# Three units of the first layer's last two groups by seven half-size products, in an attention and feed-forward kernel

## The chip, the cores and the metric

The kernel runs on one core of a Trainium2 chip. The metric is the device time of one execution in microseconds (us). Before the change four runs gave a median of 373.8 us (373.31 to 373.93). Engines: PE is the tensor engine (PEld its weight loads), DVE the vector engine, ACT the scalar engine, POOL the GpSimd engine, SP the engine that issues most transfers.

## The reference

```python
# q, k, v: (8 batches, 8 heads, 576 rows, 64); bias_table: (32, 8)
scores = 1/8 * q @ k.T + bias_table[bucket(|i - j|)]        # per batch and head
attn   = exp(scores - max) / (sum(exp(scores - max)) + 1e-9)
x      = (attn @ v) laid out as 4608 rows of 512
h      = np.maximum(x @ w_in, 0.0)                          # w_in: 512 x 2048
out    = (h * h) @ w_out                                    # w_out: 2048 x 512, out in float32
```

## The kernel before, in words

**Stages.** Attention runs over 32 pairs of heads (`pair`, four per batch). A pair makes scores on PE into two PSUM sets of two banks each (`sets_ps`, ring `r_set`), ACT takes their exponentials into one of three rooms in SBUF (`pt_sb`, ring `r_pt`), DVE multiplies in the bias bands, PE multiplies by v into the bank `pv_ps` (ring `r_pv`), DVE normalises into `xs`, and SP transposes that by DMA into `xt_sb`. The feed-forward runs over nine groups of 512 rows (`layers(g)`, g = 0 to 8). Layer 1 of a group is 16 blocks of 128 hidden units: four matmuls 512 wide per block (L1094) into one of three PSUM banks (`g_ps`, ring `r_g`), an ACT relu out of PSUM into one of four buffers `rts` (L1115), a DVE square into `gs` (L1125). Layer 2 (`second(g)`) is done by seven products of half-size blocks in place of eight: DVE sums of the squared activations (`sums_of_activations`, L971, in two chunks of four operations), each product as two runs of eight matmuls 256 wide (L1012), and evictions by ACT copies (L1045) or DVE multiply-and-adds (L1039) into `ys`, from where SP writes rows of the output (L1065).

**Order.** A planner (`Plan.schedule`) puts all operations in order before the kernel is emitted. It takes the operation that can start earliest by its own model of times; among those on one engine that can start at the same time the one with the smallest `due` goes first. The order it finds is fixed on every engine. Layer 1 of group g has dues from 60000 + 39000 g in steps of 2000; the products of `second(g - 1)` lie between them; evictions have due 0, squares the group's due less 100000, sums of activations the group's due less 50000.

**The end.** Group 7 needs rows of the last batch, group 8 only such rows. So layer 1 of groups 7 and 8 and layer 2 of groups 7 and 8 come behind the last pair. Before, the order of the seven products in the last group was

```python
P_ORDER = "1 2 6 5 7 3 4"
P_LAST = "1 6 2 5 7 3 4"
```

where products 1 and 2 need only squares, product 6 the second sum (s2, for which the first sum s1 is needed), 5 the first, 7 the third and 3 the fourth. Products 1 and 2 add up in one bank "a".

Of the kernel before, what the change touches and what calls it, by code (L numbers as in the profile page):

```python
# [10 lines left out]
FP32 = mybir.dt.float32  # L11
FP16 = mybir.dt.float16
EXPF = mybir.ActivationFunctionType.Exp
RELUF = mybir.ActivationFunctionType.Relu
COPYF = mybir.ActivationFunctionType.Copy
MULT = mybir.AluOpType.mult

# [18 lines left out]
QUIET, LATER = 5000.0, 9000  # L36
TAB, EV = 2700.0, 1
P_ORDER = "1 2 6 5 7 3 4"
P_LAST = "1 6 2 5 7 3 4"
SIX = 2  # L40
V_EARLY, V_HW = 18900.0, 2
T_POOL, T_DUE = 0, 0
ORDER = "k0 i0 q1 q0 v i1 o0 k1 i2 o1 o2 i3 o3"
HALF = GT // 2
# [135 lines left out]
def mm(n):  # L180
    return n / 2.4 + 2.5
# [6 lines left out]
def dve(n, rate=1.0, fix=160.0):  # L188
    return fix + n / (0.96 * rate)
# [3 lines left out]
def kernel(  # L193
# [415 lines left out]

    xt_ready, x_last = {}, {}  # L610
    x_bufs = {}

    def copy_to(engs_n, out_f, in_f, deps, bufs, due, fp16=True, dve_only=False):

# [13 lines left out]
    def pair(p):  # L628
# [190 lines left out]
        for part, qt0, nq in ((0, 0, 3), (1, 3, 2)):  # L819
            bank = Buf(r_pv)  # L820

            def pv(qt0=qt0, nq=nq, bank=bank):
                ps = pv_ps[bank.slot][:, 0 : nq * 130].rearrange("p (t e d) -> p t e d", t=nq, e=2)
                pt, pm = pts[pb.slot], p4s[pb.slot]
                va, vm = vas[b_v[b].slot], v4s[b_v[b].slot]
                for i in range(nq):
                    c = (qt0 + i) * 128
                    io(
                        nc.tensor.matmul(  # L829
                            ps[:, i, :, :], pm[:, c : c + 128], vm[:, hp, :, 0:65], start=True, stop=False  # L830
                        )
                    )
                    for e in range(2):
                        for jt in range(4):
                            io(
                                nc.tensor.matmul(  # L836
                                    ps[:, i, e, :],
                                    pt[:, (2 * jt + e) * S + c : (2 * jt + e) * S + c + 128],
                                    va[:, jt, 2 * hp + e, 0:65],
                                    start=False,  # L840
                                    stop=(jt == 3 and e == 1),
                                )
                            )

            o = P.add(
                {"PE": nq * 300.0}, pv,
                bands + list(exps.values()) + l_v[b, hp] + first, [bank, pb, b_v[b]], T + 1, after, "f",
            )
            rb = Buf(r_r)

            def recip(nq=nq, bank=bank, rb=rb):
                ps = pv_ps[bank.slot][:, 0 : nq * 130].rearrange("p (t e d) -> p t e d", t=nq, e=2)
                io(nc.vector.reciprocal(out=rs[rb.slot][:, 0:nq], in_=ps[:, :, :, 64:65]))

            def norm(nq=nq, bank=bank, rb=rb, qt0=qt0):
                ps = pv_ps[bank.slot][:, 0 : nq * 130].rearrange("p (t e d) -> p t e d", t=nq, e=2)
                io(
                    nc.vector.tensor_tensor(  # L858
                        out=xs[xb.slot][:, qt0 : qt0 + nq, :].rearrange("p t (e d) -> p t e d", e=2),
                        in0=ps[:, :, :, 0:64],  # L860
                        in1=rs[rb.slot][:, 0:nq].to_broadcast([128, nq, 2, 64]),
                        op=MULT,
                    )
                )

            o = P.add({"DVE": 200.0}, recip, [o], [bank, rb], T - 2000)
            o = P.add({"DVE": dve(nq * 128)}, norm, [o], [bank, rb, xb], T - 2000)
            norms.append(o)
            if b >= DT_X:
                c = (b % XB) * S + 128 * qt0  # L870
                t = P.add(
                    {"SP": 1320.0},
                    lambda qt0=qt0, nq=nq, c=c: io(
                        nc.sync.dma_start_transpose(
                            out=xt_sb[:, hp, c : c + 128 * nq].rearrange("p (t d) -> p t d", d=128), in_=xs[xb.slot][:, qt0 : qt0 + nq, :].rearrange("p t d -> p (t d)")
                        )
                    ),
                    [o, x_last.get((hp, 1 - part))] + xt_free(b * S + 128 * (qt0 + nq)), [xb], T - 2000,
                )
                t = x_last[hp, part] = P.add({"DMA": 232.0 * nq}, None, [t], [xb], -1e9)  # L880
                end = b * S + min(128 * (qt0 + nq), S) - 1
                for g_ in range((b * S + 128 * qt0) // GT, end // GT + 1):
                    xt_ready.setdefault(g_, []).append(t)
# [48 lines left out]
    def sums_of_weights():  # L932
# [21 lines left out]
            done.append(o)  # L954
        return done

    def sums_of_activations(g):

        gb = g_bufs[g]
        sb_ = s_bufs[g] = {i: Buf(r_s[i]) for i in (1, 2, 4)}  # L960
        for c0 in (0, 4):
            o = None
            for to, uses in ((1, [1]), (2, [1, 2]), (4, [2, 4]), (3, [])):

                def add(to=to, c0=c0):
# [5 lines left out]
                    io(nc.vector.tensor_tensor(out=out_, in0=a, in1=b_, op=mybir.AluOpType.subtract))  # L971

                o = P.add(
                    {"DVE": dve(1024, 2.0)}, add, squares[g][2 * c0 : 2 * c0 + 8] + [o],
                    [gb] + [sb_[i] for i in uses], G0 + GP * g - 5e4,
                )
                s_done.setdefault((g, to), []).append(o)
# [1 line left out]
    def second(g):  # L979

        gb, sb_ = g_bufs[g], s_bufs[g]
        bank = {i: Buf(r_g) for i in ("a", "b", "c", "d0")}
        bank["d1"] = Buf(r_g) if g == NG - 1 else bank["d0"]
        y = {i: Buf(r_y) for i in ("u", "v", "11", "12")}
        rows_ = out[ds(g * GT, GT), :].rearrange("(s t p) c -> t p s c", s=2, t=2)
        prod = {
            1: ("a", lambda c, s: fourth(gb, 0, 0, c, 1)[:, 0, s], lambda c: w4[:, c, 0, 0], []),
            2: ("a", lambda c, s: fourth(gb, 1, 0, c, 1)[:, 0, s], lambda c: w4[:, c, 1, 0], []),
            3: ("c", lambda c, s: ss[4][:, c, s], lambda c: w4[:, c, 1, 1], [4]),
            4: ("d", lambda c, s: fourth(gb, 1, 1, c, 1)[:, 0, s], lambda c: wt_sb[:, 2, c], []),  # L990
            5: ("c", lambda c, s: ss[1][:, c, s], lambda c: w4[:, c, 0, 1], [1]),
# [10 lines left out]
        atoms = []  # L1002
        for i in (int(x) for x in (P_LAST if g == NG - 1 else P_ORDER).split()):
            bk, left, right, ns = prod[i]
            apart = bk == "d" and g == NG - 1
            for s_ in range(2):
                bf = bank[f"d{s_}" if bk == "d" else bk]

                def mul(i=i, s_=s_, bf=bf, left=left, right=right, apart=apart):
                    for c in range(8):  # L1010
                        io(
                            nc.tensor.matmul(  # L1012
                                g_ps[bf.slot][:, ts(s_, HALF)], left(c, s_), right(c),
                                start=(c == 0 and (s_ == 0 or apart) and i not in before), stop=(c == 7),
                                skip_group_check=True,
                            )
                        )

                def atom(d, i=i, s_=s_, bf=bf, ns=ns, mul=mul):
                    deps = d + [x for n in ns for x in s_done[g, n]] + squares[g]  # L1020
                    deps += read_of[before[i]] if i in before else []
                    deps += l_wout if i in (1, 2) else t_done
                    return P.add(
                        {"PE": 8 * mm(HALF)}, mul, deps, [bf, gb] + [sb_[n] for n in ns if n != 3], 1e6, 0.0, "f",
                    )
# [2 lines left out]
                if s_ == 0 and not apart:  # L1028
                    continue

                def fin(o, i=i, bf=bf, s0=s_ if apart else 0, n=1 if apart else 2):
                    to, plus, where = reads[i]
                    cs = ds(s0 * HALF, n * HALF)

                    def ev():
                        dst, ps = ys[y[to].slot][:, cs], g_ps[bf.slot][:, cs]
                        if plus is not None:
                            io(
                                nc.vector.scalar_tensor_tensor(  # L1039
# [8 lines left out]

                    deps = [o]
                    if plus == "u":  # L1050
                        deps += read_of[1 if i == 6 else 6]
                    if plus == "v":
                        deps += read_of[5]
                    if i == 4:
# [18 lines left out]
                atoms.append(fin)  # L1073
        return atoms

    def layers(g):

        due = G0 + GP * g
# [2 lines left out]
        if g < NG:  # L1081
            g_bufs[g] = Buf(r_gb)
            gb1 = g_bufs[g]
            squares[g] = []
            for nt in range(16):
                bank = Buf(r_g)

                def f1(nt=nt, bank=bank):
# [10 lines left out]
                            )  # L1099

                atoms1.append((nt, f1, bank))
        i2 = 0
        last = None
        for i in range(16):
            if i < len(atoms1):
                nt, f1, bank = atoms1[i]
                o = P.add(
                    {"PE": 4 * mm(512)}, f1, xt_ready[g] + [l_win[nt // 4]], [bank, gb1], due + i * 2000, 0.0, "f"
                )
# [3 lines left out]
                def relu(o, bank=bank, rb=rb):  # L1113
# [4 lines left out]

                engs = {"ACT": act(512), "DVE": dve(512)} if g < RELU_DVE else {"ACT": act(512)}
                r = one_of(engs, relu, [o], [bank, rb], 0.0)  # L1120
                squares[g].append(
                    P.add(
                        {"DVE": dve(512, 2.0)},
                        lambda rb=rb, nt=nt, gb1=gb1: io(
# [6 lines left out]
                )  # L1131
            if i2 < len(atoms2):
                o = atoms2[i2]([last] if last is not None else [])
                o.due = due + i * 2000 + 1000
                last = o
                i2 += 1
                if i2 < len(atoms2) and atoms2[i2].__name__ == "fin":
                    atoms2[i2](o)
                    i2 += 1
# [49 lines left out]
```

The softmax here doesn't subtract the row's maximum and nothing guards it: scores larger than these inputs give would overflow.

## Time and profile before

| | before |
|---|---|
| median of four runs | 373.8 us |
| profiled execution, time | 374.81 us |
| profiled execution, span from first to last instruction | 373.0 us |
| granted PE clock, mean over the span | 0.995 |
| last run of matmuls of exponentials by v begins | 312.65 us |
| first layer-1 matmul of group 7 begins | 315.35 us |
| 315.35 to 357.00: busy PE, PEld, DVE, ACT | 41.65, 25.10, 24.09, 19.70 us |
| last DVE eviction begins | 369.97 us |

Times below are microseconds from the start of the profiled span. A row of groups gives line, engine, operation, output and input, shapes and count, then busy time, mean ns of one instruction, and the idle time of the engine in front of it with its releaser. A row of the chain of waits gives start, length and what ran. Records of PE overlap: a matmul's record is longer than the step from one to the next, and the steps are read from the chain.

### The profile page before, as it was taken

The page shows a single profiled execution, that of the slowest core. Times are in us where ns is not written, and L with a number is a line of the kernel's source. Part 1 is how long each engine was busy: PE and PEld are TensorE (multiplying, and loading weights), DVE is VectorE, ACT ScalarE, POOL GpSimd, SP SyncE. Part 2 cuts the span into 40 slices and gives each one's busy share as a digit, 9 for nine tenths or more (in the row PEclk, how much of TensorE's full clock was granted, in tenths as well). Part 3 has the DMA queues.
Part 4 walks back from the last instruction along what each step waited for, and adds up shares of the span by engine and source line. Part 5 has one row for each costly group of instructions (what it writes and reads, how often), then busy time and mean ns, then how long its engine had stood idle before and what let it go on. Part 6 is the DMA issues. An engine that isn't in the chain of part 4 may idle for free.

```text
span 373.0 us, 9912 instructions
## 1 busy us (share of the span) xinstructions
PE 356.9 (96%) x3930; PEld 243.1 (65%) x3930; DVE 265.6 (71%) x593; ACT 258.1 (69%) x368; POOL 184.2 (49%) x343
## 2 busy tenths in 40 slices
PE   3988999899999999999999999999999999999996
PEld 2656555656687557877785468745877688456775
DVE  3897799958785598658865697579765985583663
ACT  4988889688585886689766887688659870564330
POOL 7896358495665495666846557758413100000000
PEclk9999999999999999999999999999999999999999
DMA  9999999795998989998999899999975122100103
GB/s 171 145 133 160 171 187 105 100 111 78 190 139 108 161 133 143 138 151 155 127 138 136 112 162 128 141 176 154 88 118 129 47 55 66 56 2 28 58 28 114
DMA packets 162292, 44.25 MB, mean 119 GB/s; under 512 B 145734, under 2 KB 162246, under 8 KB 162246
## 3 DMA queue, kind: packets, MB, share of 16 engines
q0 software_dynamic: 74208, 14.53, 49.9%
q1 hardware_dynamic: 87696, 28.80, 41.1%
q8 instruction: 31, 0.51, 0.6%
q10 hardware_dynamic: 342, 0.30, 0.3%
q14 instruction: 15, 0.12, 0.1%
HBM read 36.88 MB, written 9.44 MB: 124 GB/s over the span
## 4 chain that ended last, share of the span: by engine, by line
PE 84%; DVE 6%; ACT 4%; DMA 3%; issue 1%; POOL 0%; SPq 0%; ACTq 0%
PE f L1094 33%; PE f L1012 28%; PE pv L836 8%; PE st L701 8%; PE pv L829 2%; DMA kt<-ks 2%; PE st L750 2%; DVE pt L793 2%; PE st L725 1%; DMA g<-in_q_dram 1%; ACT pt L712 1%; DVE x L858 1%; PE f L656 1%; DVE s L971 1%; ACT pm L760 1%
## 5 line engine op out<-in xcount | busy, mean ns | idle before, releaser
L712 ACT ACTIVATE pt<-st 128x1024 f16<-128x1024 f32 x128 | 127.3, 1023 | 31.5 <-PE st L701 31.5
L1094 PE MATMUL f<-xt,w_in_sb 128*128 128x512 f16 (+4 forms) x704 | 138.6, 341 | 0.2 <-ACT xt L618 0.2
L1115 ACT ACTIVATE rt<-f 128x512 f16<-128x512 f32 x144 | 85.2, 601 | 49.2 <-PE f L1094 45.2
L1094 PEld LDWEIGHTS <-w_in_sb 128*128 128x128 f16 x704 | 62.6, 98 | 57.3 <-issue 12.2
L1125 DVE TENSOR_TENSOR g<-rt 128x512 f16<-128x512 f16 x144 | 63.7, 446 | 36.1 <-ACT rt L1115 35.1
L793 DVE TENSOR_TENSOR pt<-pt,tb_sb 128x1536 f16<-128x1536 f16 (+2 forms) x96 | 60.7, 642 | 15.1 <-ACT pt L712 14.5
L1012 PEld LDWEIGHTS <-g 128*128 128x128 f16 x576 | 54.6, 98 | 14.4 <-issue 4.7
L275 POOL DMA_DIRECT2D qs<-in_q_dram x79 | 55.3, 714 | 5.1 <-DMA w_out_sb<-in_moe_w_out_dram 2.6
L275 POOL DMA_DIRECT2D ks<-in_k_dram x79 | 55.2, 702 | 1.1 <-issue 1.0
L836 PE MATMUL pv<-va,pt 128*128 128x65 f16 x1280 | 55.3, 194 | 0.0
L836 PEld LDWEIGHTS <-pt 128*128 128x128 f16 x1280 | 50.7, 98 | 3.1 <-issue 1.3
L1039 DVE SCALAR_TENSOR_TENSOR y<-f,y 128x512 f32<-128x512 f32 (+1 forms) x47 | 31.4, 667 | 24.1 <-PE f L1012 22.4
L1012 PEld LDWEIGHTS <-s 128*128 128x128 f16 x432 | 41.1, 98 | 10.5 <-issue 2.7
L701 PE MATMUL st<-qt,kt 64*128 64x512 f16 x256 | 40.9, 391 | 0.9 <-ACT pt L735 0.4
L683 POOL COPY qz<-kt 64x64 f16<-64x64 f16 x58 | 19.8, 342 | 39.8 <-DMA kt<-ks 30.2
L1012 PE MATMUL f<-w_out_sb,g 128*128 128x256 f16 x288 | 36.2, 273 | 0.7 <-ACT y L1045 0.7
L683 POOL COPY qz<-qt 64x64 f16<-64x64 f16 x61 | 16.9, 277 | 39.9 <-DMA qt<-qs 26.4
L829 PE MATMUL pv<-vm,pm 128*128 128x130 f16 x160 | 35.5, 222 | 1.0 <-DVE x L858 1.0
L1012 PE MATMUL f<-wt,g 128*128 128x256 f16 x288 | 36.2, 273 | 0.0
L1012 PE MATMUL f<-w_out_sb,s 128*128 128x256 f16 x288 | 36.1, 273 | 0.0
L858 DVE TENSOR_TENSOR x<-pv,r 128x384 f16<-128x384 f32 x64 | 31.4, 490 | 2.0
L971 DVE TENSOR_TENSOR s<-g,s 128x1024 f16<-128x1024 f16 x36 | 26.1, 724 | 0.4
(64 smaller groups left out, 283.5 us busy)
## 6 DMA issues: line engine op xcount, KB each, us to landing
out_dram<-y SPq DMA_DIRECT2D x34, 256.0 KB, 2.3
f<-in_v_dram SPq DMA_DIRECT2D x24, 256.0 KB, 4.2
qs<-in_q_dram POOLq DMA_DIRECT2D x48, 64.0 KB, 4.0
ks<-in_k_dram POOLq DMA_DIRECT2D x48, 64.0 KB, 3.5
w_in_sb<-in_moe_w_in_dram POOLq DMA_DIRECT2D x4, 512.0 KB, 7.3
w_out_sb<-in_moe_w_out_dram POOLq DMA_DIRECT2D x4, 512.0 KB, 10.4
qs<-in_q_dram POOLq DMA_DIRECT2D x7, 144.0 KB, 4.5
ks<-in_k_dram POOLq DMA_DIRECT2D x7, 144.0 KB, 6.0
```

Source lines behind the costliest of these rows:

```text
L275: lambda: io(eng.dma_start(out=out_(), in_=in_())),
L683: io(eng.tensor_copy(out=dst[qb.slot][rw, rw], in_=src[qb.slot][rw, 512:576]))
L701: nc.tensor.matmul(sets_ps[st.slot][:, e, :], kt[rw, ts(jt, 128)], qt[rw, 0:512], start=True, stop=True,)
L712: nc.scalar.activation(out=p5(pts[pb.slot])[:, jt, :, 0:512], in_=sets_ps[st.slot], func=EXPF, scale=SCALE)
L793: io(nc.vector.tensor_tensor(out=a, in0=a, in1=t, op=MULT))
L829: nc.tensor.matmul(ps[:, i, :, :], pm[:, c : c + 128], vm[:, hp, :, 0:65], start=True, stop=False)
L836: nc.tensor.matmul(ps[:, i, e, :], pt[:, (2 * jt + e) * S + c : (2 * jt + e) * S + c + 128], va[:, jt, 2 * hp + e, 0:65], start=False, sto ...
L858: nc.vector.tensor_tensor(out=xs[xb.slot][:, qt0 : qt0 + nq, :].rearrange("p t (e d) -> p t e d", e=2), in0=ps[:, :, :, 0:64], in1=rs[rb.s ...
L1012: nc.tensor.matmul(g_ps[bf.slot][:, ts(s_, HALF)], left(c, s_), right(c), start=(c == 0 and (s_ == 0 or apart) and i not in before), stop= ...
L1094: nc.tensor.matmul(g_ps[bank.slot][:, a:z], w_in_sb[:, kk, ts(nt, 128)], xt_sb[:, kk, c : c + z - a], start=(kk == 0), stop=(kk == 3),)
L1115: io(nc.scalar.activation(out=rts[rb.slot], in_=g_ps[bank.slot], func=RELUF))
L1125: nc.vector.tensor_tensor(out=gs[gb1.slot][:, nt, :], in0=rts[rb.slot], in1=rts[rb.slot], op=MULT)
```

## The change

In group 7 two units and in group 8 one unit of layer 1 are done by seven products. A unit u covers four blocks: hidden blocks 2u and 2u + 1, and 8 + 2u and 9 + 2u. With the inner dimension in two halves and the 512 rows in two halves, a unit is a product of 2 x 2 blocks. Where the old code has 4 blocks x 4 matmuls 512 wide, the new has 7 products x 4 matmuls 256 wide, into `sets_ps`. Four DVE sums of weights per unit number (`late["s"]`, made once for u = 0 and u = 1) and four DVE sums of x per group (`late["t"]`) come first; both, and the float32 partial results (`late["y"]`), lie in `pt_sb`, and wait for the last three pairs' products with v (`pv_last`). Evictions are one ACT copy, one ACT relu and five DVE multiply-and-adds per unit; three of the latter are followed by an ACT relu in place in `rts`. The squares of units may go to DVE or to ACT. The blocks that are left (8 in group 7, 12 in group 8) are done as before, at the later places of the loop in `layers`; squares are kept by block (`made` gives those of some blocks).

In the last group products 1 and 2 of layer 2 are done first, 2 in the bank `pv_ps` of its own, and its eviction is a DVE addition to product 1's in place of an ACT copy. Layer 2 of group 7 has its dues raised by 7000. The diff below is cut; its parts belong, in order, to the constants, `pair`, the list of squares, `second`, the new functions and `layers`.

```diff
+SQUAREF = mybir.ActivationFunctionType.Square
...
-P_LAST = "1 6 2 5 7 3 4"
+P_LAST = "1 2 6 5 7 3 4"
...
+LATE2 = 7000
+UNITS = {7: 2, 8: 1}
+USTEP = 700.0
...
+            if p >= 4 * B - 3:
+                pv_last.append(o)
...
+    def made(g, a, z):
+        return [x for nt in range(a, z) for x in squares[g][nt]]
...
+        bank["e"] = Buf(r_pv) if g == NG - 1 else bank["a"]
...
-            2: ("a", lambda c, s: fourth(gb, 1, 0, c, 1)[:, 0, s], lambda c: w4[:, c, 1, 0], []),
+            2: ("e", lambda c, s: fourth(gb, 1, 0, c, 1)[:, 0, s], lambda c: w4[:, c, 1, 0], []),
...
+            own = bk == "e" and g == NG - 1
+            home = pv_ps if own else g_ps
...
+                                home[bf.slot][:, ts(s_, HALF)], left(c, s_), right(c),
+                                start=(c == 0 and (s_ == 0 or apart) and (own or i not in before)), stop=(c == 7),
...
+                def fin(o, i=i, bf=bf, s0=s_ if apart else 0, n=1 if apart else 2, own=own, home=home):
...
+                    plus = "u" if own else plus
...
+                        dst, ps = ys[y[to].slot][:, cs], home[bf.slot][:, cs]
...
                     if plus == "u":
-                        deps += read_of[1 if i == 6 else 6]
+                        deps += read_of[1 if i in (2, 6) else 6]
+                    if i == 6 and g == NG - 1:
+                        deps += read_of[2]
...
+    late, r_late = {}, Ring(4)
+    def late_room():
+        a, b_, c_ = (pt_sb[:, i, 0:4096] for i in range(3))
...
+        for i in range(1, 5):
+            late["s", i] = a[:, ts(i - 1, 1024)].rearrange("p (k c) -> p k c", k=2)
+            late["y", i - 1] = b_.bitcast(FP32)[:, ts(i - 1, 512)]
+        for g in UNITS:
+            for i in range(1, 5):
+                o = ((g - min(UNITS)) * 4 + i - 1) * 512
+                late["t", g, i] = c_[:, o : o + 512].rearrange("p (k c) -> p k c", k=2)
+    def late_sums(n, dst, terms, deps, due):
+        o, made_ = None, []
+        for i, (a, b_, op) in terms:
+            o = P.add(
+                {"DVE": dve(n, 2.0)},
+                lambda i=i, a=a, b_=b_, op=op: io(nc.vector.tensor_tensor(out=dst(i), in0=a(), in1=b_(), op=op)),
+                deps + [o], (), due,
+            )
+            made_.append(o)
+        return made_
+    SUB = mybir.AluOpType.subtract
+    def by_sevens(g, units, due):
+        if not late:
+            late_room()
+        c = (g * GT) % XR
+        assert c + GT <= XR
+        wq = lambda i, k, u: w_in_sb[:, 2 * k : 2 * k + 2, 1024 * i + 256 * u : 1024 * i + 256 * u + 256]
+        xq = lambda k, j: xt_sb[:, 2 * k : 2 * k + 2, c + HALF * j : c + HALF * j + HALF]
+        t = lambda i: late["t", g, i]
+        t_ops = late_sums(
+            512, t,
+            [
+                (1, (lambda: xq(0, 1), lambda: xq(0, 0), SUB)),
+                (2, (lambda: xq(1, 1), lambda: t(1), SUB)),
+                (4, (lambda: xq(1, 0), lambda: t(2), SUB)),
+                (3, (lambda: xq(1, 1), lambda: xq(0, 1), SUB)),
+            ],
+            xt_ready[g] + pv_last, due - 1e5,
+        )
...
+        for u in range(units):
+            s_ = lambda i, u=u: late["s", i][:, :, ts(u, 256)]
+            if ("ops", u) not in late:
+                late["ops", u] = late_sums(
+                    512, s_,
+                    [
+                        (1, (lambda u=u: wq(1, 0, u), lambda u=u: wq(1, 1, u), mybir.AluOpType.add)),
+                        (2, (lambda s_=s_: s_(1), lambda u=u: wq(0, 0, u), SUB)),
+                        (4, (lambda u=u: wq(0, 1, u), lambda s_=s_: s_(2), SUB)),
+                        (3, (lambda u=u: wq(0, 0, u), lambda u=u: wq(1, 0, u), SUB)),
+                    ],
+                    l_win + pv_last, due - 1e5 + 10.0 * u,
+                )
+            sets = {"ab": Buf(r_set), "cd": Buf(r_set)}
+            y = {i: Buf(r_late) for i in "uv"}
+            prod = {
+                1: ("a", lambda u=u: wq(0, 0, u), lambda: xq(0, 0), True),
+                6: ("b", lambda s_=s_: s_(2), lambda: t(2), True),
+                2: ("a", lambda u=u: wq(0, 1, u), lambda: xq(1, 0), False),
+                5: ("c", lambda s_=s_: s_(1), lambda: t(1), True),
+                7: ("d", lambda s_=s_: s_(3), lambda: t(3), True),
+                3: ("c", lambda s_=s_: s_(4), lambda: xq(1, 1), False),
+                4: ("d", lambda u=u: wq(1, 1, u), lambda: t(4), False),
+            }
+            reads = {
+                1: ("u", None, None), 6: ("u", "u", None), 2: (None, None, (0, 0)), 5: ("v", "u", None),
+                7: (None, "v", (1, 1)), 3: (None, "u", (0, 1)), 4: (None, "u", (1, 0)),
+            }
+            after_read = {2: 1, 3: 5, 4: 7}
+            read_of = {}
+            for n, i in enumerate((1, 6, 2, 5, 7, 3, 4)):
+                bk, left, right, first_ = prod[i]
+                st = sets["ab" if bk in "ab" else "cd"]
+                ps = lambda st=st, bk=bk: sets_ps[st.slot][:, "abcd".index(bk) % 2, :]
...
+                                nc.tensor.matmul(
+                                    ps()[:, ts(f, HALF)], left()[:, kk, ts(f, 128)], right()[:, kk, :],
+                                    start=(first_ and f == 0 and kk == 0), stop=(kk == 1), skip_group_check=True,
+                                )
+                            )
+                o = f1_last[g] = P.add(
+                    {"PE": 4 * mm(HALF)}, mul,
+                    xt_ready[g] + t_ops + late["ops", u] + (read_of[after_read[i]] if i in after_read else []),
+                    [st, gb1], due + (7 * u + n) * USTEP, 0.0, "f",
+                )
+                to, plus, where = reads[i]
+                deps = [o]
+                if plus == "u":
+                    deps += read_of[1 if i == 6 else 6]
+                if plus == "v":
+                    deps += read_of[5]
+                bufs = [st] + [y[x] for x in {to, plus} - {None}]
+                rb = Buf(r_rt) if where else None
+                bufs += [rb] if rb else []
+                def ev(e, to=to, plus=plus, ps=ps, y=y, rb=rb):
+                    dst = rts[rb.slot] if rb else late["y", y[to].slot]
+                    if plus is not None:
+                        io(
+                            nc.vector.scalar_tensor_tensor(
+                                out=dst, in0=ps(), scalar=1.0, in1=late["y", y[plus].slot], op0=MULT, op1=mybir.AluOpType.add
+                            )
+                        )
+                    else:
+                        io(nc.scalar.activation(out=dst, in_=ps(), func=RELUF if rb else COPYF))
+                e = one_of({"DVE": dve(512)} if plus else {"ACT": act(512)}, ev, deps, bufs, 0.0)
...
+                if plus is not None:
+                    e = P.add(
+                        {"ACT": act(512)},
+                        lambda rb=rb: io(nc.scalar.activation(out=rts[rb.slot], in_=rts[rb.slot], func=RELUF)),
+                        [e], [rb], 0.0,
...
+                def square(o, rb=rb, where=where, u=u):
+                    src = rts[rb.slot].rearrange("p (f s) -> p f s", f=2)
+                    n0 = 8 * where[0] + 2 * u
+                    dst = gs[gb1.slot][:, n0 : n0 + 2, ts(where[1], HALF)]
+                    if o.eng == "ACT":
+                        io(nc.scalar.activation(out=dst, in_=src, func=SQUAREF))
+                    else:
+                        io(nc.vector.tensor_tensor(out=dst, in0=src, in1=src, op=MULT))
+                e = one_of({"DVE": dve(512, 2.0), "ACT": act(512)}, square, [e], [rb, gb1], due - 1e5)
...
+            squares[g] = {nt: [] for nt in range(16)}
+            units = UNITS.get(g, 0)
+            for nt in [nt for nt in range(16) if nt % 8 >= 2 * units]:
...
+            if units:
+                by_sevens(g, units, due)
...
+        skip = 16 - len(atoms1) if g < NG else 0
...
+            if i >= skip and g < NG:
+                nt, f1, bank = atoms1[i - skip]
...
-                o.due = due + i * 2000 + 1000
+                o.due = due + i * 2000 + 1000 + (LATE2 if g == NG - 1 else 0)
```

## The prediction

> **What bounds the kernel now.** I read the page first: its engine shares and its chain of work that ended last.
>
> ```profile
> span 373.0 us, 9912 instructions
> PE 356.9 (96%) x3930; PEld 243.1 (65%) x3930; DVE 265.6 (71%) x593; ACT 258.1 (69%) x368; POOL 184.2 (49%) x343
> PE 84%; DVE 6%; ACT 4%; DMA 3%; issue 1%; POOL 0%; SPq 0%; ACTq 0%
> ```
>
> PE holds 84% of the chain, but that is a mean over stages. Nothing that the change adds can start before the last pairs' products with v, so I read the end by itself: the busy time by stretch (columns: length, then busy time and count of PE, PEld, DVE, ACT, POOL, then the clock).
>
> ```profile
> 315.35:357.00 41.65, 41.65 (x259) 25.10 (x257) 24.09 (x50) 19.70 (x33) 0.00 (x0) 1.00 0.14 46
> 313.60:359.20 45.60, 45.60 (x294) 28.47 (x291) 26.48 (x54) 20.60 (x35) 0.00 (x0) 1.00 0.14 44
> ```
>
> From the first layer-1 matmul of group 7 to the last of group 8 PE has no idle time at all, at full clock. DVE and ACT are busy for 58% and 45% of it. A microsecond taken out of PE here is a microsecond off the end, if no new wait appears. The chain of waits, in order of time, gives the prices of matmuls and the one place where PE is not the bound (start, length, what):
>
> ```profile
> 312.90 2.62 PE f L1012 x24
> ...
> 319.85 12.95 PE f L1094 x60
> ...
> 354.53 2.60 PE f L1094 x12
> 357.13 0.02 issue
> 357.15 0.61 ACT rt L1115
> 357.76 0.02 issue
> 357.78 0.44 DVE g L1125
> 358.22 0.02 issue
> 358.24 0.70 DVE s L971
> 358.94 0.02 issue
> 358.97 0.70 DVE s L971
> 359.67 0.05 issue
> 359.72 10.23 PE f L1012 x92
> ```
>
> A matmul 512 wide takes 12.95 / 60 = 0.2158 us, one 256 wide, with a weight load of its own each time, 2.62 / 24 = 0.1092. The only wait of PE in the last 60 us is in front of the second half of product 6 of group 8, which needs the sum s2: last block, relu, square, s1, s2. In the waits of PE it is 0.42 us:
>
> ```profile
> PE f L1012 <- DVE s L971: 0.4, 1, 0.4
> ```
>
> For the rest I take the groups from 313 to 361 us (busy, mean ns, idle before):
>
> ```profile
> L1125 DVE TENSOR_TENSOR g<-rt 128x512 f16<-128x512 f16 x32 | 13.6, 424 | 16.9 <-ACT rt L1115 16.8
> L1039 DVE SCALAR_TENSOR_TENSOR y<-f,y 128x512 f32<-128x512 f32 x8 | 5.5, 688 | 2.1 <-DMA xt<-x 1.1 <-PE f L1012 0.9
> L1115 ACT ACTIVATE rt<-f 128x512 f16<-128x512 f32 x32 | 19.1, 597 | 28.1 <-PE f L1094 27.8 <-DVE g L971 0.3
> ```
>
> DVE's and ACT's idle time is waiting for PE's next block: they have room, and the rows give the price of what is added.
>
> **PE: the units.** A unit takes out 4 blocks x 4 = 16 matmuls of 0.2158 = 3.453 us and puts in 7 x 4 = 28 of 0.1092 = 3.058 us. The form is that of layer 2's products, whose step holds with weights and moving data from different tiles, so I take the same price. Gain 0.395 us each, 1.19 us for three.
>
> **PE: the last group's order.** With product 2 second, products 1 and 2 (2 x 16 x 0.1092 = 3.50 us) lie between the last block and product 6, where before only product 1 (1.75 us) did. Before, s2 was done 359.67 - 356.95 = 2.72 us after PE left the last block. 3.50 covers this by 0.78 us, so the wait of 0.42 goes. Next late is product 5 (s1, done earlier than s2), then 7, with 1.75 us more each: nothing. Product 2 in a bank of its own needs an addition on DVE (0.69) in place of an ACT copy. DVE is idle for 2.74 us in front of its eviction at 364.73, so it hides. Product 6's eviction has to wait for it; product 5, behind it on PE, uses another bank. The last products 7, 3, 4 and what follows the last matmul stay as they are.
>
> **DVE: sums and evictions.** Added are 8 sums of weights and 8 of x, each 512 elements in fp16 like the squares: 16 x 0.424 = 6.8 us. Each unit adds five evictions: 15 x 0.69 = 10.4 us. The 12 squares of units replace 12 old ones, on DVE or ACT. DVE then has 26.5 + 17.2 = 43.7 us of work from 313.6 to 359.2 if it keeps all squares, or 43.7 - 12 x 0.424 = 38.6 if ACT takes those of units: 85 to 96% of 45.6 us. At 0.34 us from start to start, squares in a row are closer than their records, so the true load is somewhat lower. This is the tightest resource, and the reason why I add something for new waits below.
>
> **ACT.** 12 relus go, and 15 operations of the same size come (per unit a copy, a relu, three relus in place): 20.6 + 3 x 0.6 = 22.4 us, 29.6 with all 12 squares, of 45.6. There is room. What is queued in order behind a relu that waits for a DVE eviction is the next block's relu; PE feels that only when its three banks are full.
>
> **Waits that the change adds.** Sums of weights wait for the last matmul with v (ends about 312.9). They run in DVE's gap up to 317 (before, it holds two multiply-and-adds of 0.69 and one square). Sums of x need the transposes of the last pair, as PE's first block at 315.35 does: 4 x 0.42 puts the first unit product at about 317.2. Until then PE has two blocks of group 7 and the last product of group 6's layer 2 (two runs of 0.87) ready. If that cover were gone, it would cost 317.2 - 315.35 = 1.85 us once. Inside a unit the chain product 1, copy, evictions 6, 5, 7, 3, 4 is 0.44 + 0.60 + 5 x 0.69 = 4.5 us against 3.06 us of PE. PE falls back on the 20 remaining blocks (20 x 0.863 = 17.3 us), and these use other banks than the units: three units need about 3 x 1.4 = 4.3 us of that. SP and POOL get no new transfers; a y stored late by DVE delays only an output.
>
> The price of new waits lies between 0 (all of this is covered) and three times the chain's surplus plus the late start, 4.3 + 1.85 = 6.2 us. The nearest row is the end's own wait of 0.42 us, the one place in this stage where DVE was not in time. I take half of it, 0.2 us, since more DVE work makes some such place likely while the fill is large. Below nothing is excluded: PE has no other idle time to give back.
>
> **Square on ACT.** The trace shows one load of activation tables in the whole run (L316, 1.283 us), with exponential, relu and copy all served. It shows no Square. If it were in another set, each ACT square could bring two loads, 2.6 us. I take 0. The Trainium skill ("ScalarE: Activation LUTs", "Table sets: the hidden batching unit") says that cheap functions are in every set, but names relu, copy, identity and abs, not square. As an estimate from that page's 2.66 us for each switch (section "What ACT_TABLE_LOAD costs"), 12 squares would cost ACT up to 64 us. No row here shows a switch.
>
> **A rule against the change.** The trace has 512 elements on DVE at 0.424 and 1024 at 0.686 us: about 0.16 us of each is fixed, 31 added operations pay 5 us of it, and 43.7 above contains it. The Trainium skill ("VectorE: DVE Perf Modes", "Rules for kernel authors") says to minimize the number of operations rather than semaphores. By that rule alone 17 us of small DVE work for 1.2 us of PE is a bad trade; by the rows it is paid from idle time.
>
> **Sum.** -1.19 - 0.42 + 0.2 = -1.4 us. The profiled execution (span 373.0, time 374.81) would become 371.6 and 373.4; the median of runs lies 1.0 below that execution, so 373.8 - 1.4 = 372.4. Without any new wait 372.2. The forecast's own range is 371.9 to 373.0.
>
> **Rivals.**
>
> 1. *The units' chains eat the gain.* The planner's order is fixed; with sets, four rt buffers and DVE all shared, PE waits some 0.5 us for each unit's evictions (one DVE operation of 0.69 in the way, partly hidden). For: 4.5 us of chain against 3.06 of PE. Against: 17.3 us of other blocks. Price 3 x 0.5: -1.61 + 1.5 gives 373.7, no change that can be told.
> 2. *DVE becomes the bound of the tail (slower).* By 359.26 (355.76, when PE is through, + 3.50) DVE must have done s2, that is 43.7 less the last two sums, 42.3 us since 313.6. So 45.66 - 42.3 = 3.4 us is all the idle time that it may have when it keeps all squares, 8.5 when ACT takes them. Before it was idle for 19.1 us in that stretch, mostly waiting for relus. If it keeps 60% of that waiting, 11.5 us, with half the squares on ACT (5.9 allowed), product 6 comes 5.6 us late, part of which early sums give back; I price it at +4 net of this: -1.61 + 4 gives 376.2. It decides from about 7.5 us of idle on DVE. Against: the layer-2 products of group 7, which PE can take later by the raised dues, let DVE catch up where it now idles most (335 to 345 us).
> 3. *Square isn't in the loaded set.* ACT would have 29.6 + up to 24 x 1.283 = 60.4 us in 45.6: +15, or 387.
> 4. *The end's wait does not go*, since the last sums come later than I think: -1.19 + 0.2, 372.8, inside the range.
>
> **How the numbers follow.** A measurement of this kernel can tell about 0.2%, 0.75 us, from no change: faster is below 373.05, slower above 374.55. Forecast with rival 4: 0.66. Rival 1: 0.15. Rival 2: 0.16, of which 0.01 ends within 0.2%. Rival 3: 0.03. So faster 0.66, same 0.16, slower 0.18. The range goes from 371.9 (no new wait, and 0.3 for the spread of medians) to 375.2, which takes in rival 1 and the mild half of rival 2 and leaves out about 0.12 above.
>
> **What would show it.** Right: layer-1 rows of 84 matmuls 256 wide stepping at 0.109; PE without idle from 315.35 to the last block; the last block's end about 1.2 us earlier; no wait of product 6 for DVE; one table load. Wrong: a row of PE waits on evictions over 0.5 us in sum (rival 1); PE waiting for sums of activations near the end with DVE above 95% (rival 2); table loads in the tail (rival 3). A first layer-1 matmul of group 7 that is no longer at 315.35 would mean that the order in front of it changed, which I take as untouched.

## The result and the profile after

The changed kernel takes 374.84 us (median of 44 runs, 373.77 to 376.92), the kernel before 373.72 us (63 runs). The ratio is 1.0030, 95% interval 1.0022 to 1.0039: 1.1 us slower. The forecast was 1.4 us faster.

The page of the changed kernel (engine shares with instruction counts, then the engines of the chain that ended last):

```profile
span 372.3 us, 10016 instructions
PE 355.1 (95%) x3966; PEld 245.7 (66%) x3966; DVE 277.1 (74%) x619; ACT 261.4 (70%) x376; POOL 186.7 (50%) x343
PE 87%; DVE 7%; ACT 4%; DMA 1%; issue 1%; ACTq 0%; DVEq 0%
```

The span is shorter than before (373.0) though the kernel is slower. The two profiled executions differ ahead of the change: the first layer-1 block of group 7 starts at 313.54 us here and at 315.35 before, with the same PE order up to the first unit and a mean granted clock of 1.0 here and 0.995 there. So spans mislead, and I compare the stretch from that block to the start of the last run of 16 matmuls on PE. It was 368.02 - 315.35 = 52.67 us before and is 367.32 - 313.54 = 53.78 us now: +1.11, which is the whole result. The rows of PE (the first is of the profile before, the others of the changed kernel's):

```profile
368.02 1.91 PE L1012 MATMUL f<-wt,g 128*128 128x256 f16 x16
...
313.54 1.03 PE L1258 MATMUL f<-xt,w_in_sb 128*128 128x512 f16 x4
...
367.32 1.91 PE L1027 MATMUL f<-wt,g 128*128 128x256 f16 x16
```

The waits of PE from 290 us on, and the busy time (length, PE, PEld, DVE, ACT) of the stretch that the prediction showed:

```profile
PE st L1183 <- DVE pt L1208: 1.1, 2, 0.6
PE st L1183 <- DVE rt L1208: 0.6, 1, 0.6
313.60:359.20 45.60, 43.73 (x315) 30.59 (x314) 37.94 (x77) 24.59 (x44) 0.00 (x0) 1.00 0.13 42
```

L1183 is a product of a unit, L1208 the DVE eviction of another product. PE now stands still inside units, while neither DVE (37.9 of 45.6 us) nor ACT (24.6) is full. PE in order of time, in the two units of group 7 (start, length of the records, line, operation, tiles, shape, count, idle before):

```profile
317.00 0.60 PE L1183 MATMUL st<-xt,w_in_sb 128*128 128x256 f16 x4
317.44 1.47 PE L1183 MATMUL st<-pt 128*128 128x256 f16 x12
319.50 0.60 PE L1183 MATMUL st<-xt,w_in_sb 128*128 128x256 f16 x4 [0.59 <-DVE pt L1208]
...
325.35 0.60 PE L1183 MATMUL st<-xt,w_in_sb 128*128 128x256 f16 x4
325.79 1.04 PE L1183 MATMUL st<-pt 128*128 128x256 f16 x8
326.66 1.03 PE L1258 MATMUL f<-xt,w_in_sb 128*128 128x512 f16 x4
328.33 0.60 PE L1183 MATMUL st<-xt,pt 128*128 128x256 f16 x4 [0.64 <-DVE rt L1208]
328.76 1.03 PE L1258 MATMUL f<-xt,w_in_sb 128*128 128x512 f16 x4
329.78 0.60 PE L1183 MATMUL st<-pt,w_in_sb 128*128 128x256 f16 x4
```

A unit starts with product 1 (317.00), then 6, 5, 7 (x12 at 317.44). Product 2 could follow at 317.44 + 12 x 0.1092 = 318.75, but starts at 319.50. By start times and the steps 0.1092 and 0.2158, seven places are open: in front of product 2 by 0.75, 0.21 and 0.70 us (three units), of product 3 by 0.81 and 0.21, of product 4 by 0.16 and 0.07; in all 2.91 us. (The waits above, 1.7 us, count only from the modelled end of a matmul's record.)

Product 2 uses bank a and by its data has to wait only for the ACT copy out of bank a. What ACT and DVE did at that time:

```profile
317.20 0.60 ACT L1282 ACTIVATE rt<-f 128x512 f16<-128x512 f32 x1 [0.27 <-PE f L1258]
318.12 0.60 ACT L1213 ACTIVATE pt<-st 128x512 f32<-128x512 f32 x1 [0.33 <-PE st L1183]
318.75 1.49 DVE L1208 SCALAR_TENSOR_TENSOR pt<-st,pt 128x512 f32<-128x512 f32 x2 [0.50 <-ACT pt L1213]
```

Product 2 started at 319.50, 0.05 us after the first of the two evictions, that of product 6 out of bank b, was over (318.75 + 0.69). The copy ended at 318.72, so with the same 0.05 us it alone would have held up product 2 by some 0.03 us. The copy itself came late too: product 1 had left PE at 317.44 and ACT was free from 317.80 on, but the copy started at 318.12, 0.25 us behind product 6 (317.87). Banks a and b are the two halves of one tile of `sets_ps`. The program's own list of instructions has the wait (line, operation, output and inputs):

```
L1183 Matmult st1_119<-xt_99,w_in_sb_62 128x256 [waits DVE_49]
```

This is product 2's first matmul; it waits for the semaphore that DVE counts up, though only ACT reads its bank in front of it.

### The profile page after: what moved, and what is told of

The parts are those of the page before. It is cut to its first block, busy times and chain, and to the rows that moved or that the text cites. A ratio compares the mean times of both kernels' runs of the same rounds, so it can differ in the third digit from the quotient of the medians.

```text
span 372.3 us, 10016 instructions
## 1 busy us (share of the span) xinstructions
PE 355.1 (95%) x3966; PEld 245.7 (66%) x3966; DVE 277.1 (74%) x619; ACT 261.4 (70%) x376; POOL 186.7 (50%) x343
## 4 chain that ended last, share of the span: by engine, by line
PE 87%; DVE 7%; ACT 4%; DMA 1%; issue 1%; ACTq 0%; DVEq 0%
PE f L1258 31%; PE f L1027 28%; PE pv L841 9%; PE st L706 8%; PE pv L834 3%; PE st L755 2%; PE st L1183 2%; PE st L730 2%; ACT pt L717 1%; DMA g<-in_q_dram 1%; PE f L661 1%; DVE x L865 1%; DVE pt L798 1%; DVE pt L1208 1%; ACT pm L765 1%; PE f L362 1%
## 5 line engine op out<-in xcount | busy, mean ns | idle before, releaser
L1258 PE MATMUL f<-xt,w_in_sb 128*128 128x512 f16 (+4 forms) x656 | 127.5, 338 | 0.2 <-ACT xt L623 0.2
L1282 ACT ACTIVATE rt<-f 128x512 f16<-128x512 f32 x132 | 77.8, 601 | 34.2 <-PE f L1258 30.1
L1258 PEld LDWEIGHTS <-w_in_sb 128*128 128x128 f16 x656 | 57.9, 98 | 52.7 <-issue 12.2
L1292 DVE TENSOR_TENSOR g<-rt 128x512 f16<-128x512 f16 x132 | 58.4, 450 | 21.2 <-ACT rt L1282 20.4
L1027 PEld LDWEIGHTS <-s 128*128 128x128 f16 x432 | 41.2, 98 | 9.0 <-issue 2.5
L688 POOL COPY qz<-qt 64x64 f16<-64x64 f16 x61 | 20.7, 339 | 39.6 <-DMA qt<-qs 29.1
L688 POOL COPY qz<-kt 64x64 f16<-64x64 f16 x58 | 18.5, 318 | 34.9 <-DMA kt<-ks 26.5
L1027 PE MATMUL f<-w_out_sb,g 128*128 128x256 f16 x272 | 34.5, 273 | 0.7 <-ACT y L1061 0.7
```

The lines of the kernel that those rows point to most:

```text
L688: io(eng.tensor_copy(out=dst[qb.slot][rw, rw], in_=src[qb.slot][rw, 512:576]))
L1027: nc.tensor.matmul(home[bf.slot][:, ts(s_, HALF)], left(c, s_), right(c), start=(c == 0 and (s_ == 0 or apart) and (own or i not in before ...
L1258: nc.tensor.matmul(g_ps[bank.slot][:, a:z], w_in_sb[:, kk, ts(nt, 128)], xt_sb[:, kk, c : c + z - a], start=(kk == 0), stop=(kk == 3),)
L1282: io(nc.scalar.activation(out=rts[rb.slot], in_=g_ps[bank.slot], func=RELUF))
L1292: nc.vector.tensor_tensor(out=gs[gb1.slot][:, nt, :], in0=rts[rb.slot], in1=rts[rb.slot], op=MULT)
```

## Experiments

**Theories.** A: a matmul into one bank, and a reader of it, wait for the other bank of the same two-bank tile too; the planner, which goes by the data, doesn't know and leaves nothing else to do in that place. B: the chain of evictions of a unit is too long in itself. C: DVE is full, and waits only moved.

**Banks paired otherwise (e1_pairs).** Products 1, 2 and 7, 4 share a tile; 6 and 5, 3 the other.

```diff
-            sets = {"ab": Buf(r_set), "cd": Buf(r_set)}
+            sets = {"ad": Buf(r_set), "bc": Buf(r_set)}
...
-                st = sets["ab" if bk in "ab" else "cd"]
-                ps = lambda st=st, bk=bk: sets_ps[st.slot][:, "abcd".index(bk) % 2, :]
+                st = sets["ad" if bk in "ad" else "bc"]
+                ps = lambda st=st, bk=bk: sets_ps[st.slot][:, "abcd".index(bk) // 2, :]
```

> The changed kernel with its four unit banks paired otherwise in the two sets: products 1, 2 and 7, 4 share one two-bank tile, 6 and 5, 3 the other. Theory A (a reader or writer of one bank waits for the other bank of the same two-bank tile, so product 2 waits for the eviction of 6, product 3 for that of 7, and the copy of 1 for the matmuls of 6): the gaps of PE inside units, 2.9 us in the changed kernel's profile, fall below 0.8 us, and the time falls by about 2 us to 372.5 to 373.0. Theory B (the chain of evictions itself is too long for what PE has to do beside it): the pairing changes nothing, gaps stay at 2 to 3 us and the time at 374.8. Theory C (DVE is full at the end): the gaps move behind the units, to product 6 of the last group, time 374 to 375.

Measured: 372.50 us against 373.59 of the kernel before on the same chip, ratio 0.9964 (0.9948 to 0.9980). PE in order of time:

```profile
318.57 0.60 PE L1183 MATMUL st<-xt,w_in_sb 128*128 128x256 f16 x4
319.00 1.50 PE L1183 MATMUL st<-pt 128*128 128x256 f16 x12
320.34 0.60 PE L1183 MATMUL st<-xt,w_in_sb 128*128 128x256 f16 x4
320.77 1.89 PE L1258 MATMUL f<-xt,w_in_sb 128*128 128x512 f16 x8
...
329.83 0.60 PE L1183 MATMUL st<-pt,w_in_sb 128*128 128x256 f16 x4 [0.20 <-DVE rt L1208]
```

The first unit has the same order as in the changed kernel (1, then 6, 5, 7, then 2), and product 2 follows at 319.00 + 1.31 = 320.31 without the gap of 0.75. In this unit work and order are the same and only the pairing differs: B falls, A stands. (The later units come in another order here, so for them the run alone doesn't tell.) The stretch is 51.45 us. What is left are 0.35 us in front of product 4 at 329.83 and 0.16 behind the units.

**The planner told (e2_told).** The tiles and waits as in the changed kernel, but as dependencies for the planner.

```diff
-            after_read = {2: 1, 3: 5, 4: 7}
+            after_read = {2: (1, 6), 3: (5, 7), 4: (7, 3)}
...
-                    xt_ready[g] + t_ops + late["ops", u] + (read_of[after_read[i]] if i in after_read else []),
+                    xt_ready[g] + t_ops + late["ops", u] + [x for r in after_read.get(i, ()) for x in read_of[r]],
...
+                for r in {6: (1,), 7: (5,)}.get(i, ()):
+                    read_of[r][0].deps.append(o)
```

> The changed kernel, with the planner told that product 2 of a unit waits for the evictions of 1 and 6, product 3 for those of 5 and 7, 4 for those of 7 and 3, and the evictions of 1 and 5 for the matmuls of 6 and 7; the waits on the chip are what they were, only the order may change. Theory A: the planner puts other blocks into the places where PE stood, gaps inside units fall below 0.8 us, time 372.5 to 373.2. Theory B: the planner already had other work to put there and the gaps stay above 2 us, 374.5 to 375. Theory C: gaps inside units fall, but PE waits for sums at the end instead, 374 to 375.

Measured: 372.56 us, ratio 0.9979 (0.9967 to 0.9990). PE:

```profile
318.13 1.47 PE L1183 MATMUL st<-pt 128*128 128x256 f16 x12
319.44 1.89 PE L1260 MATMUL f<-xt,w_in_sb 128*128 128x512 f16 x8
321.17 0.60 PE L1183 MATMUL st<-xt,w_in_sb 128*128 128x256 f16 x4
...
347.82 1.48 PE L1027 MATMUL f<-wt,s 128*128 128x256 f16 x12 [0.44 <-DVE s L982]
```

Two blocks now stand where PE was idle, and no unit has a gap. There was other work all along; only the order lacked it. The stretch is 51.50 us. One wait is new, for group 7's sums at 347.82 (0.60 us by start times): a small part of C. So theory A has two halves: the tiles make the waits, and a planner that doesn't know of them leaves PE idle in them.

**The last group's order alone (e3_last_only).** `UNITS = {}`, `LATE2 = 0`.

> No units and no raised dues; only the last group's order 1 2 6 5 7 3 4 with product 2 in its own bank. All theories: the 0.42 us wait of product 6 goes, and nothing else moves: 0.3 to 0.5 us faster than before, 373.3. If the price of this part was wrong, it is 0 or slower.

Measured: 373.33 us, ratio 0.9990 (0.9976 to 1.0004); the interval holds both 0 and the forecast. The trace decides: product 6 no longer waits, and the stretch is 52.08 us, 0.59 below before. The wait was worth 0.58 us by start times (359.72 - 358.70 - 4 x 0.1092), not the 0.42 that the waits list.

**The units without that order (e4_units_only).** `P_LAST` and product 2's bank as before.

> The units and the raised dues, with the last group's order and bank as before the change. In the changed kernel's profile the last layer-1 block ends 8.7 us before the last group's product 1, so the sums are done long before: undoing the order should cost nothing, and the time is that of the changed kernel, 374.8 (within 0.2). If the order's 0.42 us is separate from the units, it is 375.2.

Measured: 374.89 us, ratio 1.0036 (1.0024 to 1.0048), the stretch 53.77 us, as in the changed kernel. With the raised dues, layer 2 of group 7 lies between the last block and the last group and covers the sums by itself. The two parts of the change don't add: the order's gain is had once.

**Product 6 in a tile of its own (e5_own6).** In the old pairing:

```diff
+            six = Buf(r_pv)
...
+                if i == 6:
+                    st, ps = six, lambda six=six: pv_ps[six.slot][:, :]
```

> The changed kernel with product 6 of each unit in the bank pv_ps, a tile of its own, and the rest as it was (1, 2 alone in one set; 5, 3 and 7, 4 together in the other). Theory A (the wait follows the two-bank tile): product 2's gaps (0.75, 0.21, 0.70 us in the changed kernel's profile) go, those of products 3 and 4 (0.81, 0.16, 0.21, 0.07) stay; time 374.8 - 1.6 = 373.2. If the wait did not follow the tile, or the new pairing of the run before helped for another reason (another order), nothing changes: 374.8. If everything goes, 372.3, the gaps of 3 and 4 were a consequence of those of 2.

Measured: 373.51 us, ratio 0.9996 (0.9978 to 1.0014), the stretch 52.43 us, 1.35 below the changed kernel's.

```profile
318.86 0.60 PE L1186 MATMUL st<-xt,w_in_sb 128*128 128x256 f16 x4
...
327.49 0.60 PE L1186 MATMUL st<-xt,pt 128*128 128x256 f16 x4 [0.64 <-DVE rt L1211]
...
338.15 0.60 PE L1186 MATMUL st<-xt,pt 128*128 128x256 f16 x4 [0.36 <-DVE rt L1211]
```

All three gaps of product 2 are gone, those of products 3 and 4 stay (0.81, 0.16, 0.53, 0.07). One of them grew, from 0.21 to 0.53, so 1.34 us of gaps went and not the 1.66 of product 2. In the instruction list product 2's first matmul now waits for ACT alone:

```
L1186 Matmult st1_119<-xt_99,w_in_sb_62 128x256 [waits Activation_49]
```

The wait follows the tile, product by product.

**Four units (e6_pairs4).** The new pairing with `UNITS = {7: 2, 8: 2}`.

> The new pairing of banks (products 1, 2, 7, 4 in one tile, 6, 5, 3 in the other) with four units, two in each group. If PE stays the bound, the fourth unit is worth the price of matmuls, 16 x 0.2158 - 28 x 0.1092 = 0.40 us: 372.1. If DVE (17 us more work than before for three units, 3.9 more for the fourth) becomes the bound, PE waits for sums and the time rises, to 373 or more.

Measured: 374.11 us, ratio 1.0012 (0.9997 to 1.0027); the stretch is 52.78 us, 1.33 above that of three units.

```profile
346.09 0.71 PE L1027 MATMUL f<-w_out_sb,g 128*128 128x256 f16 x5
348.36 1.38 PE L1027 MATMUL f<-w_out_sb,g 128*128 128x256 f16 x11 [1.56 <-ACT g L1231]
```

PE has run out of blocks. It begins the last group's product 1 at 346.09 and waits in it 1.7 us for a square of the last unit, made on ACT, at the end of the chain eviction, relu, square. Group 7's other products couldn't fill the place: DVE began the second half of their sums only at 347.90. With four units C is true in this order: evictions, relus and squares, not PE, hold up this stage. Four units with the planner told of the waits were not run.

**Without the raised dues (e7_pairs_late0).** The new pairing, `LATE2 = 0`.

> The new pairing with three units, without the raised dues of layer 2 of group 7. If the raised dues give DVE the time that it needs, PE now waits for the sums of group 7 or 8 and the time rises by 0.3 to 1 us, to about 373. If the order finds enough other work by itself, it is the same, 372.5.

Measured: 373.07 us, ratio 0.9972 (0.9952 to 0.9993). The median looks like the slower forecast, but 5 of its 12 runs had a mean clock of 0.994 or 0.995; the other seven have a median of 372.06, and the six such runs of e1_pairs 372.09. The stretch is 51.44 us, that of the new pairing. The raised dues do nothing here: also without them the last five products of group 7 lie behind the last block (from 346.42 us on).

**New pairing and the planner told of its waits (e8_pairs_told).**

```diff
+            after_read = {2: (1,), 7: (1,), 3: (5, 6), 4: (7, 2)}
...
+                for r in {5: (6,)}.get(i, ()):
+                    read_of[r][0].deps.append(o)
```

> The new pairing with three units, and the planner told of the waits that this pairing has: the eviction of 6 waits for the matmuls of 5, product 7 for the copy of 1, 4 for the reads of 7 and 2. In the run with the new pairing alone 0.5 us of gaps are left from the first block of group 7 on (51.45 us from there to the last run of matmuls, 52.67 in the kernel before). Theory A: they go, the stretch becomes about 51.0 us and the time 371.9 to 372.3. If the rest has another cause (late DVE sums, the order behind the units), it stays at 51.4 and 372.5.

Measured: 372.38 us against 373.90, ratio 0.9961 (0.9944 to 0.9978), 1.5 us below before. By the times it can't be told from the new pairing alone (0.9964); by the stretch, 51.16 us, it is 0.29 shorter, two thirds of the way to A's forecast. The list shows no wait of PE from 300 us on, but by start times one gap of 0.26 is left, in front of product 4 of the first unit. That waits for the eviction of 7, which DVE began at 321.83, behind the ACT relu of product 2.

**One unit (e9_one_unit).** The changed kernel with `UNITS = {7: 1}`.

> The changed kernel with its banks as they are and one unit, in group 7, in place of three. Theory A (0.7 to 1 us of gaps for each unit from the shared tiles, against 0.40 us of matmuls saved): gaps of 0.7 to 1.1 us, stretch from the first block of group 7 to the last run of matmuls 52.08 - 0.40 + 0.9 = 52.6 us, time 373.6 to 373.9. If the cost of units were one of crowding (DVE or ACT too full with three of them), one unit alone would have no gaps: 51.7 us and 372.9.

Measured: 373.91 us, ratio 0.9999 (0.9985 to 1.0013). The gaps are 0.75, 0.22 and 0.08 us in the one unit, the stretch 52.73 us. Each unit brings its own gaps, about 1 us; crowding isn't needed for them.

**All runs on one sum.** Work on PE is 0.8632 us for a block (4 x 0.2158), 0.4368 for a unit's product (4 x 0.1092), 0.8736 for half a product of layer 2 (8 x 0.1092); the rest are the gaps read in the trace.

| kernel | work | gaps | sum | measured stretch | ratio of times |
|---|---|---|---|---|---|
| before | 52.08 | 0.58 | 52.66 | 52.67 | 1 |
| last group's order alone | 52.08 | 0 | 52.08 | 52.08 | 0.9990 |
| one unit | 51.69 | 1.05 | 52.74 | 52.73 | 0.9999 |
| changed kernel | 50.90 | 2.91 | 53.81 | 53.78 | 1.0030 |
| units without that order | 50.90 | 2.91 | 53.81 | 53.77 | 1.0036 |
| product 6 apart | 50.90 | 1.57 | 52.47 | 52.43 | 0.9996 |
| banks paired otherwise | 50.90 | 0.51 | 51.41 | 51.45 | 0.9964 |
| the same, without raised dues | 50.90 | 0.53 | 51.43 | 51.44 | 0.9972 |
| the same, four units | 50.50 | 2.26 | 52.76 | 52.78 | 1.0012 |
| planner told | 50.90 | 0.60 | 51.50 | 51.50 | 0.9979 |
| paired otherwise and planner told | 50.90 | 0.26 | 51.16 | 51.16 | 0.9961 |

## Why the prediction was wrong

- **Price of units: right.** 52.08 - 50.90 = 1.18 us of PE work went, forecast 1.19.
- **The end's wait: right in kind, undersized, and not the order's doing.** It went, worth 0.58 and not 0.42. In the changed kernel the order of the last group has no part in it (e4_units_only); layer 2 of group 7 covers it.
- **New waits: the step that failed.** The term was 0.2 us and measured 2.91. I took the deps written in the new functions for the waits on the chip and concluded that PE falls back on blocks that use other banks. Those deps are what the planner sees. The waits are put in later and follow tiles, and units put four independent banks into two tiles. The blocks to fall back on were there (e2_told uses them), but with an order fixed ahead PE can't fall back on anything at a wait that the planner doesn't know. The bounds (0 to 6.2) held the value. The choice between them did not: a wait elsewhere in the stage says nothing about a new sharing of tiles. The late start, 1.85 us of those bounds, cost nothing: the first unit began without a gap, at 317.00.
- **Rival 1: right in kind, half in price.** It had PE wait for one DVE operation of 0.69 per unit, "partly hidden", 0.5 us, and so no change that can be told, 373.7. The gaps of the three units are 0.75, 1.18 and 0.98 us, so the time is 374.84; the large gaps are about an eviction each. Its sign came: 1.7 us of PE waits on evictions. What the rival gave as its cause, shared sets, was the cause; the length of the chain was not (e1_pairs has the same chain).
- **Rival 2: not at three units, in part at four.** DVE's load was forecast at 38.6 to 43.7 us (41.2 with the 6 of 12 squares that ACT took) and was 37.9; ACT 24.6 in a forecast of 22.4 to 29.6. PE lacked no sums in the changed kernel; with a fourth unit it lost 1.7 us to a late square, not to a sum. The raised dues, which I held against this rival, did nothing (e7_pairs_late0).
- **Rival 3: didn't occur.** The whole run still has one load of tables:

```profile
L320 ACT ACT_TABLE_LOAD x1 | 1.3, 1283 | 2.6 <-issue 2.6
```

- **The sum.** -1.18 - 0.58 + 2.91 = +1.15; measured +1.11 in the stretch, +1.12 in the medians. That 374.84 lies within 371.9 to 375.2 is no merit of the mechanism: the upper part was there for the rivals. The forecast itself, 372.4, went the wrong way.
- **A slip in reading.** ACT's 45% is its share of the longer stretch; from the first to the last layer-1 matmul it was 19.70 of 41.65 us, 47%. Nothing rests on it.
- **The sign that I named for a changed order, a first block not at 315.35,** was a bad one: it starts at 313.54 with the same order, 1.8 us earlier because this execution ran faster in front of it (its clock between 20 and 100 us was 1.00, that of the profile before 0.98).

The Trainium skill ("PSUM — Partial Sum Buffer", "PSUM bank collisions raise a hardware error") asks for a guard by bank and quadrant, and says that accesses of two engines to different banks run clean. The waits found here are wider than that, by tiles of two banks. No run here took such a wait away while keeping two independent banks in one tile, so whether the chip would need it was not tried.

## What to carry to other kernels

When an order is planned ahead, price a new sharing of a buffer by what the program will wait for, which here is the tile, and not by the data: list each tile with two independent chains in it and add, for each, one operation of the other chain. If the waits can't go, tell the planner of them: with the same tiles and waits, e2_told won back 2.3 us of the stretch by order alone. To compare two profiled executions, take a stretch that starts behind what both share, not the span.

## What the runs showed of the hardware

- Executions of one program differ by their granted clock. Of the changed kernel's 44 runs 34 had a mean clock of 0.999 or 1.0 and a median of 374.7 us, ten had 0.995 and 376.1. In the two profiles with a mean of 0.995 (before, e1_pairs) the clock was 0.98 between 20 and 100 us and 1.00 in the rest. A difference of 1.4 us between two single profiles is as large as what this change does.
- ACT on 512 elements took 0.624 us from SBUF (the relu in place, L1222, float16) and 0.592 to 0.598 from PSUM (L1282, L1213, float32).
- The list of waits counted the end's wait of 0.58 us as 0.42, because a matmul's record (0.272 us) ends about 0.16 us behind the step to the next (0.109).
